# Early attention scores in pairs of sets on four 64x64 array tiles, value tiles kept by head pair, and a planner with other durations

## The chip, the cores and the metric

The kernel runs on one core of a Trainium2 chip. The metric is the device time of one launch in microseconds. The kernel before takes 553.24 us (median of 3 runs, 553.12 to 553.94).

## The reference, cut to what matters

Inputs: q, k, v of shape (2, 8, 768, 64): batch, heads, sequence, head width. Three stages follow one another, all in fp32.

```python
# 1. attention: banded local keys plus 24 summary keys (one for each block of 32)
k_sum = k.reshape(B, H, 24, 32, D).max(axis=3)
v_sum = v.reshape(B, H, 24, 32, D).mean(axis=3)
scores = concat(where(|i - j| < 16, scale * q @ k.T, -1e9), scale * q @ k_sum.T + log(32))
a = softmax(scores); x = a @ concat(v, v_sum)        # then (1536 tokens, 512)
# 2. h = x @ w_in (512 x 2048); g = h * tanh(softplus(h)); y = g @ w_out (2048 x 512)
# 3. out = ((y @ w1) * (y @ w2)) @ w3 @ w_out2
```

## The kernel before, in words

**Dense work.** The 1536 tokens are three blocks of 512 (n = 0, 1, 2). Each fp32 product of the dense stages is made of three matmuls on high and low parts (`mm3`, L103 to L106). Stage 2 goes by chunks of 128 hidden columns: `hidden` (12 matmuls of 128x512, written h) and `project` (12 more, written y). The weights come as 1 MB DMAs of 64-bit words and are decoded by `list_weight`: `shrink` (ACT or POOL), `low`, `sign` and `join` (DVE), `hi` (ACT) and `lo` (DVE), written c, dc.

**Attention.** One set is 256 tokens of one pair of heads of one batch: 24 sets in the order of `SETS`. A set has four groups of 64 queries; each sees 96 local keys and 24 summary keys, so a score row has 120 columns (`KW`). Sets 0 to 7 (`early`) are batch 0, tokens 0 to 511: together block n = 0, which the first h matmuls need. Sets 8 to 11 are (0, hp, 2), sets 12 to 15 (1, hp, 0), and sets 16 to 23 are (1, hp, 1) and (1, hp, 2), head pair by head pair.

- Early sets: keys of the whole batch lie in the tile `k`, queries in `qp`. `score` (L963) issues for each group and head one matmul on 96 keys and one on the 24 summary keys. The query group is the 64x64 weight; the two heads use the upper and the lower half of the array and write the two halves of the partitions of one PSUM bank. The banks are a ring of two (`a_ring`), one bank for a set.
- Late sets come in pairs: `score_two` (L978) writes the two heads to two banks and the two groups of a pair to the two halves of partitions, so that four 64x64 tiles of the array are in use. Their queries, keys and values come in one DMA (`load_late`, 624 KB) into `lt`, one of four tiles; `widen_k` and `widen_v` (POOL) write the 24 summary columns and rows beside them.
- After the scores: `peak` (DVE, four mask-and-max instructions, each with a read of its accumulator), `expo` (ACT, four exps), `invert` (DVE), `norm` (POOL), `turn_p` (PE, four transposes), `store_p` (ACT or DVE), `attend` or `attend_two` (PE), `store_x` (high part on ACT, low part on DVE; xh, xl).
- Summary values of batch 0: `parts_v` (PE, pn), `store_parts` (ACT, vq), `join_v` (PE, pm), `store_vm` (DVE, vm), `spread_v` (POOL). `peak_k` (DVE, km) makes the summary keys. The last four value groups of batch 0 are loaded by `load_vb` (256 KB) into the end of the same tile as the queries.

**Order.** No engine chooses at run time: each executes its instructions in the order in which they are issued. `op` lists every step with an engine, a duration, the keys it reads and writes, and a rank. `issue` then plans: a backward pass (`latest`) gives each step a latest start, a forward pass (`forward`) lets each engine take the ready step with the earliest one; eight rounds, the best is issued. All durations are the numbers in the `op` calls; `wait_after` holds the hand-over times between engines. While PE has had no h matmul yet, planned idle time is filled with `warm` matmuls on zeros; 12 more (`WARM`) stand at the start. The first 18 DMAs go in the written order `QUEUE`; all DMAs are issued by SP, in order.

Of the kernel before, what the change touches and what calls it, by code (L numbers as in the profile page):

```python
# [23 lines left out]
WARM = 12  # L24
# [40 lines left out]
def fused_kernel(  # L65
# [208 lines left out]
    def list_weight(key, u, rank, due, seng, heng, leng):  # L274
# [52 lines left out]
        op("pool" if seng == "pool" else "act", 1.1, due, [k], [d], shrink, table="exp" if prelu else None)  # L327
# [34 lines left out]
    def hidden(i, hbank):  # L362
# [443 lines left out]
    mask = cp.tile([P, 4, KW], F32, name="mask")  # L806
# [8 lines left out]
    def constants():  # L815
# [80 lines left out]
    def load_vb(hp):  # L896

        nc.sync.dma_start(out=vbs[hp].rearrange("p g d -> p (g d)"), in_=vw_d[hp, :, 8 * P:12 * P])

    def load_qp(hp):  # L900
        t = cp.tile([P, LW], F32, tag=f"lt{hp}", name=f"qp{hp}", bufs=1)
        qps[hp], vbs[hp] = t[:, 0:TB], t[:, LW - TB:].rearrange("p (g d) -> p g d", d=P)
        nc.sync.dma_start(out=qps[hp], in_=q_d[hp])

    def load_late(s):

        t = cp.tile([P, LW], F32, tag=f"lt{s % RS}", name=f"lt{s}", bufs=1)
# [58 lines left out]

    def score(s, key):
        sv = st[s]["sv"] = bank(key, f"s{s}")[:, 0:4 * KW].rearrange("p (g j) -> p g j", j=KW)
        b, hp, j = sets[s]
        for i in range(4):  # L970
            c = 256 * j + 64 * i
            for h in range(2):
                hs = slice(64 * h, 64 * h + 64)
                for c0, c1, x in ((0, 96, kts[b, hp][hs, c:c + 96]), (96, KW, kms[b, hp][hs])):
                    nc.tensor.matmul(
                        sv[hs, i, c0:c1], lhsT=qps[hp][hs, c:c + 64], rhs=x, start=True, stop=True,
                        skip_group_check=True,
                    )  # L978

    def score_two(s, keys):  # L980

        two = [bank(k, f"s{s}h{h}")[:, 0:4 * KW].rearrange("p (g j) -> p g j", j=KW) for h, k in enumerate(keys)]
        for w in range(2):
            x = st[s + w]
            x["sv"] = two
            for i in range(4):
                m, r = divmod(i, 2)
                for h in range(2):
                    hs = slice(64 * h, 64 * h + 64)
                    nc.tensor.matmul(  # L990
                        two[h][64 * r:64 * r + 64, 2 * w + m], lhsT=x["q"][hs, 64 * i:64 * i + 64],
                        rhs=x["k"][hs, i, :], start=True, stop=True, skip_group_check=True,
                    )

    def peak(s):
# [4 lines left out]
        for i in range(4):  # L1000
            if early(s):
                src, y = x["sv"][:, i, :], 1 if 4 * sets[s][2] + i else 0
            else:
                g = 4 * sets[s][2] + 2 * (i % 2)
                src, y = x["sv"][i // 2][:, 2 * (s % 2) + i % 2], {0: 2, 10: 3}.get(g, 1)
# [35 lines left out]
    def attend(s, key):  # L1041
        xb = bank(key, f"x{s}")
        b, hp, j = sets[s]
        for i in range(4):
            for h in range(2):
# [4 lines left out]
                    rhs=st[s]["pt"][:, i, hs], start=True, stop=True,  # L1050
# [51 lines left out]
    def list_keys(b, hp, rank, key):  # L1102
        kt = kt_key[b, hp] = held.get(key, key)
        op("dma", 1.1 if b else 1.15, rank, [], [kt], load_k, key, b, hp, late=QUEUE.get(f"k{b}{hp}"))
        op("dve", 0.9, rank, [kt], [("km", b, hp)], peak_k, b, hp)

    def list_means(b, hp, rank, ring):
# [6 lines left out]
        else:  # L1114
            op("dma", 0.75, rank, [], [("lt", hp)], load_qp, hp, late=QUEUE.get(f"q{hp}"))
            op("dma", 1.4, rank, [], [("va", hp)], load_va, hp, late=QUEUE.get(f"va{hp}"))
            op("dma", 0.72, rank, [("lt", hp)], [("ltv", hp)], load_vb, hp, late=QUEUE.get(f"vb{hp}"))
            k0, vq = ring.get(), ("vq", hp % 2)
            op("pe", 0.82, rank + 1.0, [("va", hp), ("lt", hp), ("ltv", hp), held["k0", hp]], [k0], parts_v, hp, k0)
            op("act", 0.3, rank + 1.0, [k0], [vq], store_parts, hp)  # L1120
            op("pe", 0.3, rank + 1.0, [vq], [key], join_v, hp, key)
        if b:
            op("act", 0.25, rank, [key], [("vm", b, hp), ("vmt", hp)], store_vm, b, hp)
        else:
            op("dve", 0.25, rank + 1.0, [key], [("vmt", hp)], store_vm, b, hp)
            op("pool", 1.4, rank + 1.0, [("vmt", hp), ("va", hp), held["k0", hp]], [("vm", b, hp)], spread_v, hp)

    def list_loads(s, rank):
        op("dma", 1.65, rank, [], [("lt", s % RS)], load_late, s)

    def list_score(s, rank, ring):
        if early(s):
            b, hp, j = sets[s]
            ks = [ring.get()]
            op("pe", 1.2, rank, [kt_key[b, hp], ("km", b, hp), ("lt", hp)], ks, score, s, ks[0])
            list_soft(s, rank, ks)
            return
# [25 lines left out]
    def list_attend(s, rank, ring):  # L1163
# [6 lines left out]
        else:  # L1170
            v = [(k, x % RS) for x in (s, s + 1) for k in ("lt", "ltv")]
            op("pe", 1.25, rank, [pt_key(s), pt_key(s + 1), *v], [kx], attend_two, s, kx)
        xs = {("x", n, hp)} if e else {("x", n, hp), ("x", n, place(s + 1)[1])}
        for part, eng in ((0, "act"), (1, "dve")):
# [3 lines left out]
            cost = ((0.34, 0.59), (0.42, 0.69))[part][not e]  # L1178
# [418 lines left out]
    def list_leave():  # L1597
        ks = [(x, i) for x in ("lt", "ltk", "ltv", "sc") for i in range(RS)] + [(x, i) for x in ("mx", "sm") for i in range(EARLY)]
# [19 lines left out]
    for s, t in enumerate(when):  # L1618
# [4 lines left out]
        second = not e and s % 2  # L1623
# [69 lines left out]
def layout(q, k, v, w_in, w_out, w1, w2, w3, w_out2):  # L1693
# [27 lines left out]
    for n in range(ng):  # L1721
# [4 lines left out]
            vw[b, hp, :, 4 * j:4 * j + 4].reshape(P, TB),  # L1726
# [6 lines left out]
        "late": late,  # L1733
        "v8": np.ascontiguousarray(v8.swapaxes(3, 4)).reshape(B, HP, P, 7 * P),
# [20 lines left out]
```

## Time and profile before

| | us |
|---|---|
| median of 3 runs | 553.24 |
| the profiled execution's own time | 555.6 |
| its span, first to last instruction | 553.9 |
| PE busy | 540.4 (98%) |
| DVE busy | 412.0 (74%) |
| ACT busy | 295.8 (53%) |
| POOL busy | 137.3 (25%) |
| mean granted PE clock, as a share of full speed | 0.997 |

How to read it: the profiled execution took 555.6 us by the clock that times the runs, 1.7 us more than its span. Matmuls are pipelined, so that the busy time of PE holds overlaps; its idle time is real. The chain that ended last consists of PE for 92%. A line such as L975 is a line of the kernel file; SPq is the queue from which DMAs are issued.

### The profile page before, as it was taken

How to read it: one execution, taken by the hardware profiler on the slowest of the kernel's cores; microseconds unless marked ns; L12 is line 12 of the kernel's file. 1: busy time of each engine (PE TensorE's matmuls, PEld its weight loads, DVE VectorE, ACT ScalarE, POOL GpSimd, SP SyncE). 2: the span in 40 equal slices, each digit the busy share in tenths (PEclk: the TensorE clock that was granted, in tenths of full speed). 3: DMA queues.
4: the chain of work that ended last, by engine and by line, in shares of the span. 5: the costliest groups of instructions: out<-in, count | busy, mean ns of one | idle time of the engine just before them, and what ended most of it. 6: DMA issues, size and time to landing. Idle time of an engine off the chain costs nothing.

```text
span 553.9 us, 8388 instructions
## 1 busy us (share of the span) xinstructions
PE 540.4 (98%) x3248; PEld 442.9 (80%) x3248; DVE 412.0 (74%) x682; ACT 295.8 (53%) x552; POOL 137.3 (25%) x156
## 2 busy tenths in 40 slices
PE   8969899999999999999999999999999999999997
PEld 7747678877888888888888888888888888888885
DVE  5899886233399994357798989799667588789892
ACT  4877698597643342336343447555345654434531
POOL 4662343222223135411511200000017333500000
PEclk9998999999999999999999999999999999999999
DMA  8996722222372000030406464422261342000003
GB/s 318 417 395 215 295 95 97 90 93 94 134 323 77 0 1 0 1 152 1 149 4 227 181 275 151 153 76 77 76 235 69 115 125 100 41 2 0 1 19 133
DMA packets 13863, 69.34 MB, mean 125 GB/s; under 512 B 1536, under 2 KB 1536, under 8 KB 8192
## 3 DMA queue, kind: packets, MB, share of 16 engines
q1 hardware_dynamic: 13824, 68.82, 33.2%
q8 instruction: 25, 0.41, 0.3%
q14 instruction: 14, 0.11, 0.1%
HBM read 65.67 MB, written 3.15 MB: 124 GB/s over the span
## 4 chain that ended last, share of the span: by engine, by line
PE 92%; DMA 2%; POOL 2%; DVE 2%; issue 1%; SPq 0%; POOLq 0%
PE y L104 8%; PE y L106 8%; PE y L105 8%; PE h L104 5%; PE h L105 5%; PE h L106 5%; PE s0g L549 3%; PE s0g L548 3%; PE wc L106 3%; PE wc L104 3%; PE s0g L547 3%; PE wc L105 3%; PE pt L1034 2%; PE z L1454 2%; PE z L1453 2%; PE z L1452 2%
## 5 line engine op out<-in xcount | busy, mean ns | idle before, releaser
L519 POOL TENSOR_TENSOR dw12p<-dw12p 128x256 f32<-128x256 f32 x32 | 33.5, 1047 | 132.5 <-DVE w12p L322 127.0
L393 DVE TENSOR_TENSOR gl<-e,gh 128x512 fp32r<-128x512 f32 x32 | 24.3, 764 | 39.7 <-ACT gh L389 39.7
L104 PE MATMUL h<-xh,c 128*128 128x512 f32 x128 | 52.4, 409 | 0.0
L104 PE MATMUL y<-gh,c 128*128 128x512 f32 x128 | 51.4, 401 | 0.0
L105 PE MATMUL h<-xl,c 128*128 128x512 f32 x128 | 50.4, 394 | 0.0
L106 PE MATMUL h<-xh,c 128*128 128x512 f32 x128 | 50.3, 393 | 0.0
L106 PE MATMUL y<-gh,c 128*128 128x512 f32 x128 | 50.0, 391 | 0.0
L105 PE MATMUL y<-gl,c 128*128 128x512 f32 x128 | 49.9, 390 | 0.0
L385 ACT ACTIVATE e<-h 128x512 f32<-128x512 f32 x32 | 19.2, 600 | 56.9 <-PE h L106 56.8
L1027 POOL TENSOR_TENSOR sc<-sc,sm 128x480 f32<-128x480 f32 x24 | 27.3, 1140 | 53.8 <-DVE sm L1023 31.9
L1015 ACT ACTIVATE sc<-sc,mx 128x120 f32<-128x120 f32 x96 | 36.6, 383 | 6.8 <-DVE mx L1006 6.7
L317 ACT CAST w<-dw 128x1024 fp32r<-128x1024 f32 x20 | 20.9, 1052 | 21.6 <-DVE dw L310 21.5
L104 PEld LDWEIGHTS h<-xh,c 128*128 128x128 f32 x128 | 24.3, 190 | 5.8 <-issue 0.8
L106 PEld LDWEIGHTS h<-xh,c 128*128 128x128 f32 x128 | 24.3, 190 | 5.3
L104 PEld LDWEIGHTS y<-gh,c 128*128 128x128 f32 x128 | 24.0, 188 | 5.4 <-issue 0.7
L106 PEld LDWEIGHTS y<-gh,c 128*128 128x128 f32 x128 | 24.0, 188 | 5.2
L105 PEld LDWEIGHTS h<-xl,c 128*128 128x128 f32 x128 | 24.3, 190 | 4.5
L105 PEld LDWEIGHTS y<-gl,c 128*128 128x128 f32 x128 | 24.1, 188 | 4.5
L310 DVE SCALAR_TENSOR_TENSOR dw<-dw,w 128x1024 int32<-128x1024 int32 x20 | 25.1, 1265 | 2.1 <-ACT dw L288 1.9
L788 DVE TENSOR_TENSOR ya<-y,ya 128x512 f32<-128x512 f32 x32 | 21.7, 687 | 6.6 <-PE y L106 6.5
L104 PE MATMUL wc<-w,w 128*128 128x512 f32 x64 | 24.9, 389 | 0.0
L105 PE MATMUL wc<-w,w 128*128 128x512 f32 x64 | 24.9, 389 | 0.0
(582 smaller groups left out, 1549.6 us busy)
## 6 DMA issues: line engine op xcount, KB each, us to landing
w<-in_w SPq DMA_DIRECT2D x20, 1024.0 KB, 4.9
c<-in_w SPq DMA_DIRECT2D x16, 1024.0 KB, 11.1
lt<-in_late SPq DMA_DIRECT2D x16, 624.0 KB, 4.8
w12p<-in_w SPq DMA_DIRECT2D x8, 1024.0 KB, 5.0
k<-in_vw SPq DMA_DIRECT2D x4, 512.0 KB, 8.7
out<-c SPq DMA_DIRECT2D x8, 256.0 KB, 2.0
v<-in_v SPq DMA_DIRECT2D x4, 448.0 KB, 8.5
k<-in_kt SPq DMA_DIRECT2D x4, 400.0 KB, 6.2
```

What stands on the lines that cost most here:

```text
L104: nc.tensor.matmul(o, lhsT=lh, rhs=rh, start=start, stop=False)
L105: nc.tensor.matmul(o, lhsT=lh, rhs=rl, start=False, stop=False)
L106: nc.tensor.matmul(o, lhsT=ll, rhs=rh, start=False, stop=stop)
L310: nc.vector.scalar_tensor_tensor(out=a, in0=a, scalar=3, in1=words(T["raw"])[0], op0=ALU.logical_shift_left, op1=ALU.bitwise_or,)
L317: (nc.scalar.copy if heng == "act" else nc.vector.tensor_copy)(t[:, 0], T["a"])
L385: nc.scalar.activation(T["e"], hb(), AF.Mish)
L393: nc.vector.tensor_tensor(out=T["gl"], in0=T["e"], in1=T["gh"].bitcast(F32), op=ALU.subtract)
L519: nc.gpsimd.tensor_tensor(out=quarter(o), in0=quarter(x), in1=quarter(y), op=sign)
L547: nc.tensor.matmul(B[b], lhsT=lh, rhs=yq[r][:, 0, kk], start=first and kk == 0, stop=False, skip_group_check=True)
L788: nc.vector.tensor_tensor(out=yacc[n][:, m], in0=banks[f"y{nm}_{m}"], in1=yacc[n][:, m], op=ALU.add)
L1015: nc.scalar.activation(x["sc"][:, i, :], x["sc"][:, i, :], AF.Exp, bias=x["mx"][:, i:i + 1], scale=-1.0, accum_out=sm[:, i:i + 1],)
L1027: nc.gpsimd.tensor_tensor(out=sc, in0=sc, in1=sm.unsqueeze(2).broadcast_to([P, 4, KW]), op=ALU.mult)
```

## The change

The early sets are scored in pairs by `score_two` too, two banks for a pair, with a 96-column and a 24-column matmul for each group and head; `attend` and `peak` read the new places, and the mask has three planes in place of four. The values leave the `lt` tile: each head pair has a value tile of its own (`vbs[hp]`), loaded by `load_vb` (96 partitions) for batch 0 and by the new `load_v` (192 KB) for batch 1; sets 8 to 11 find theirs there already, and `widen_v` runs for sets 8 to 15 alone. The last eight sets go token group by token group. The planner gets other durations, a term `port` for DVE and POOL steps that overlap, a start of `expo` 0.4 before the planned end of `peak`, and 9 in place of 12 first warm matmuls. Cut to the core:

```diff
-LOW = 0.7
+LOW = 0.6
+PORT = {"low", "sign", "join", "lo"}
-WARM = 12
+WARM = 9
-SETS += [(1, hp, j) for hp in range(HP) for j in (1, 2)]
+SETS += [(1, hp, j) for j in (1, 2) for hp in range(HP)]
-LW = 256 + 4 * KW + TB
+LW = 256 + 4 * KW
...
@@ forward
-            free[e] = end = t + ops[i][1]
+            end = t + ops[i][1]
+            if e == "pool" or e == "dve" and ops[i][5].__name__ in PORT:
+                end += max(0.0, min(end, port["dve" if e == "pool" else "pool"]) - t)
+                port[e] = end
+            free[e] = end
...
-                ready[d] = max(ready[d], end + wait_after(e, g))
+                ready[d] = max(ready[d], end + (-0.4 if ops[d][5].__name__ == "expo" and e == "dve" else wait_after(e, g)))
...
@@ list_weight
-            op("dve", 1.22, due, [k], [x], sign)
-        op("dve", 1.22, due, [k, x], [d], join)
-        op(heng, 0.98 if heng == "act" else 0.62, due, [d], [k], hi)
-        op(leng, 1.4 if leng == "dve" else 2.4, due, [d], [k], lo)
+            op("dve", 1.14, due, [k], [x], sign)
+        op("dve", 1.14, due, [k, x], [d], join)
+        op(heng, 0.96 if heng == "act" else 0.62, due, [d], [k], hi)
+        op(leng, 1.14 if leng == "dve" else 2.4, due, [d], [k], lo)
...
-        nc.sync.dma_start(out=vbs[hp].rearrange("p g d -> p (g d)"), in_=vw_d[hp, :, 8 * P:12 * P])
+        nc.sync.dma_start(out=vbs[hp][0:96].rearrange("p g d -> p (g d)"), in_=vw_d[hp, 0:96, 8 * P:12 * P])
...
-        qps[hp], vbs[hp] = t[:, 0:TB], t[:, LW - TB:].rearrange("p (g d) -> p g d", d=P)
+        qps[hp] = t[:, 0:TB]
+        vbs[hp] = cp.tile([P, 4, P], F32, tag=f"lv{hp}", name=f"vb{hp}", bufs=1)
...
-        st[s]["v"] = t[:, LW - TB:].rearrange("p (g d) -> p g d", d=P)
+        st[s]["v"] = vbs[s % RS]
...
+    def load_v(s):
+        b, hp, j = sets[s]
+        nc.sync.dma_start(
+            out=vbs[hp][0:96].rearrange("p g d -> p (g d)"), in_=v1_d[hp, j]
+        )
...
-        nc.gpsimd.tensor_copy(st[s]["v"][96:KW], vms[b, hp][96:KW].unsqueeze(1).broadcast_to([NB, 4, P]))
+        nc.gpsimd.tensor_copy(vbs[hp][96:KW], vms[b, hp][96:KW].unsqueeze(1).broadcast_to([NB, 4, P]))
...
@@ score_two (score is taken out)
+            b, hp, j = sets[s + w]
+            for n in range(16 if early(s) else 8):
+                h, r, m, y = n % 2, n // 2 % 2, n // 4 % 2, n // 8
+                i, hs = 2 * m + r, slice(64 * h, 64 * h + 64)
+                o = two[h][64 * r:64 * r + 64, 2 * w + m]
+                if early(s):
+                    c = 256 * j + 64 * i
+                    q = qps[hp][hs, c:c + 64]
+                    o = (o[:, 0:96], o[:, 96:KW])[y]
+                    k = (kts[b, hp][hs, c:c + 96], kms[b, hp][hs])[y]
+                else:
+                    q, k = x["q"][hs, 64 * i:64 * i + 64], x["k"][hs, i, :]
+                nc.tensor.matmul(o, lhsT=q, rhs=k, start=True, stop=True, skip_group_check=True)
...
-        op("dma", 1.1 if b else 1.15, rank, [], [kt], load_k, key, b, hp, late=QUEUE.get(f"k{b}{hp}"))
-        op("dve", 0.9, rank, [kt], [("km", b, hp)], peak_k, b, hp)
+        op("dma", 1.1 if b else 1.15 + 1.35 * (hp == 1), rank, [], [kt], load_k, key, b, hp, late=QUEUE.get(f"k{b}{hp}"))
+        op("dve", 0.86, rank, [kt], [("km", b, hp)], peak_k, b, hp)
...
@@ list_loads
-        op("dma", 1.65, rank, [], [("lt", s % RS)], load_late, s)
+        op("dma", 1.0, rank, [], [("lt", s % RS)], load_late, s)
+        if sets[s][0]:
+            op("dma", 0.55, rank + 0.01, [], [("lv", s % RS)], load_v, s)
...
@@ list_score
-            op("pool", 0.35, rank, [("lt", i), ("km", b, hp)], [("ltk", i)], widen_k, x)
-            op("pool", 0.8, rank, [("lt", i), ("vmt", hp)], [("ltv", i)], widen_v, x)
+            op("pool", 0.23, rank, [("lt", i), ("km", b, hp)], [("ltk", i)], widen_k, x)
+            if x < EARLY + 2 * HP:
+                op("pool", 0.58, rank, [("vmt", hp)], [("lvm", i)], widen_v, x)
...
-        op("pe", 1.2, rank, reads, ks, score_two, s, ks)
+        op("pe", 1.6 if early(s) else 1.2, rank, reads, ks, score_two, s, ks)
...
-        op("dve", 0.9, rank, ks, [small("mx", s), sc_key(s)], peak, s)
-        op("act", 1.68, rank, [small("mx", s)], [sc_key(s), small("sm", s)], expo, s, table="exp")
+        op("dve", 0.82, rank, ks, [small("mx", s), sc_key(s)], peak, s)
+        op("act", 1.53, rank, [small("mx", s)], [sc_key(s), small("sm", s)], expo, s, table="exp")
...
-        op("pool", 1.1, rank, [sm], [sc], norm, s)
+        op("pool", 0.95, rank, [sm], [sc], norm, s)
...
-            v = [(k, x % RS) for x in (s, s + 1) for k in ("lt", "ltv")]
+            v = [(k, x % RS) for x in (s, s + 1) for k in ("lv", "lvm")]
...
```

## Rows read from the trace of the kernel before

**Rows 1.** The page: busy time of each engine
```profile
PE 540.4 (98%) x3248; PEld 442.9 (80%) x3248; DVE 412.0 (74%) x682; ACT 295.8 (53%) x552; POOL 137.3 (25%) x156
```
**Rows 2.** Windows: stretch, length, busy PE, PEld, DVE, ACT, POOL, clock, DMA, GB/s
```profile
8.90:25.30 16.40, 15.79 (x345) 13.49 (x346) 13.33 (x80) 14.01 (x63) 8.51 (x8) 1.00 1.03 416
25.30:46.10 20.80, 15.65 (x208) 11.86 (x208) 19.71 (x43) 16.45 (x43) 14.59 (x14) 0.92 0.77 314
60.90:68.90 8.00, 6.11 (x30) 3.79 (x28) 5.81 (x6) 4.07 (x7) 5.50 (x6) 1.00 0.62 236
...
41.40:45.00 3.60, 3.35 (x10) 2.56 (x10) 3.60 (x4) 2.11 (x3) 3.54 (x4) 0.53 0.07 27
...
500.00:554.00 54.00, 50.29 (x222) 41.29 (x220) 40.21 (x49) 21.20 (x29) 0.00 (x0) 1.00 0.10 39
```
**Rows 3.** Chain of waits, in order of time: start us, us, what
```profile
11.04 1.26 PE s L975 x29
...
45.19 0.98 PE s10h L990 x32
```
**Rows 4.** Timeline to 24 us: start us, us, engine, line, operation, idle before
```profile
1.12 4.27 PE L813 MATMUL warm<-zero 128*128 128x128 f32 x24 [1.12 <-DVE zero L817]
3.81 0.95 DVE L916 TENSOR_REDUCE km<-k 128x24 f32<-128x768 f32 x1 [0.81 <-DMA k<-in_kt]
5.32 0.39 PE L975 MATMUL s<-k,qp 64*64 64x96 f32 x4
7.07 0.95 DVE L916 TENSOR_REDUCE km<-k 128x24 f32<-128x768 f32 x1 [2.31 <-DMA k<-in_kt]
7.94 0.27 DVE L1006 CUSTOM_DVE_ANT_0 sc<-s,mask 128x120 f32<-128x120 f32 x1
...
23.73 0.08 DVE L1006 DVE_READ_ACCUMULATOR2_ANT mx<- 128x1 f32 x1
```
**Rows 5.** Waits, of DVE to 70 us, of SP to 150: total, times, longest
```profile
DVE sc L1006 <- PE s L975: 1.5, 3, 0.6
...
SPq L911 <- PE x L1061: 66.5, 6, 19.4
```
**Rows 6.** Timeline of PE, 28 to 42 us: three of its five idle stretches
```profile
28.43 0.69 PE L1048 MATMUL x<-pT,k 120*64 120x64 f32 x16 [0.57 <-POOL k L954]
...
39.99 0.65 PE L1034 MATMUL pt<-ident,sc 128*120 128x128 f32 x4 [2.36 <-POOL sc L1027]
41.65 1.11 PE L1034 MATMUL pt<-ident,sc 128*120 128x128 f32 x4 [1.01 <-POOL sc L1027]
```
**Rows 7.** Timelines of POOL and DVE: norm of a set, lo of a weight
```profile
11.63 0.99 POOL L1027 TENSOR_TENSOR sc<-sc,sm 128x480 f32<-128x480 f32 x1 [6.12 <-ACT vq L941]
30.27 1.95 POOL L1027 TENSOR_TENSOR sc<-sc,sm 128x480 f32<-128x480 f32 x1
38.13 1.81 POOL L1027 TENSOR_TENSOR sc<-sc,sm 128x480 f32<-128x480 f32 x1 [3.20 <-ACT sc L1015]
40.67 2.01 DVE L322 TENSOR_TENSOR c<-dc,c 128x1024 fp32r<-128x1024 f32 x1
58.34 1.19 DVE L322 TENSOR_TENSOR c<-dc,c 128x1024 fp32r<-128x1024 f32 x1
```
**Rows 8.** The stop after 60 us: timelines of PE and POOL, chain of waits
```profile
62.84 0.65 PE L1034 MATMUL pt<-ident,sc 128*120 128x128 f32 x4 [1.32 <-POOL sc L1027]
65.78 0.65 PE L1034 MATMUL pt<-ident,sc 128*120 128x128 f32 x4 [0.57 <-POOL sc L1027]
...
60.88 0.52 POOL L965 COPY lt<-km 128x96 f32<-128x96 f32 x1 [15.85 <-DMA lt<-in_late]
...
52.73 8.00 DMA lt<-in_late
```
**Rows 9.** Timeline of PE, 138 to 140 us
```profile
138.48 0.40 PE L104 MATMUL h<-xh,c 128*128 128x512 f32 x1
139.96 1.15 PE L1061 MATMUL x<-pT,lt 120*64 120x64 f32 x32
```

More of the change, by code (lines that the diff above doesn't have):

```diff
@@ L71, in fused_kernel @@
     late_d: bass.AP,
+    v1_d: bass.AP,
     v8_d: bass.AP,
@@ L164, in forward @@
         idle = True
+        port = {"dve": 0.0, "pool": 0.0}
         def rank_of(i):
@@ L326, in list_weight @@
         prelu = seng == "prelu"
-        op("pool" if seng == "pool" else "act", 1.1, due, [k], [d], shrink, table="exp" if prelu else None)
+        op("pool" if seng == "pool" else "act", 1.06, due, [k], [d], shrink, table="exp" if prelu else None)
         x = ("low", *k)
@@ L396, in hidden @@
         R = i + 0.9
-        op("act", 0.53, R, [hbank], [e], s0, table="mish")
-        op("act", 0.56, R, [hbank], [gh], s1, table="mish")
-        op("dve", 0.66, R, [e, gh], [gl], s2)
+        op("act", 0.5, R, [hbank], [e], s0, table="mish")
+        op("act", 0.5, R, [hbank], [gh], s1, table="mish")
+        op("dve", 0.6, R, [e, gh], [gl], s2)
         return T
@@ L805, in fused_kernel @@
     ident = cp.tile([P, P], F32, name="ident")
-    mask = cp.tile([P, 4, KW], F32, name="mask")
+    mask = cp.tile([P, 3, KW], F32, name="mask")
     cw = cp.tile([96, 2 * NB + 6], F32, name="cw")
@@ L833, in constants @@
             )
-        for i in (0, 2, 3):
+        for i in (0, 2):
             nc.vector.tensor_copy(mask[:, i, :], mask[:, 1, :])
-        nc.vector.memset(mask[:, 0, 0:WIN], NEG / scale)
-        nc.vector.memset(mask[0:64, 2, 0:WIN], NEG / scale)
-        nc.vector.memset(mask[64:P, 3, 96 - WIN:96], NEG / scale)
+        nc.vector.memset(mask[0:64, 0, 0:WIN], NEG / scale)
+        nc.vector.memset(mask[64:P, 2, 96 - WIN:96], NEG / scale)
         def bands(t, n, lo, step):
@@ L965, in widen_k @@
         nc.gpsimd.tensor_copy(st[s]["k"][:, :, 96:KW], kms[b, hp].unsqueeze(1).broadcast_to([P, 4, NB]))
[L967 to L978, printed above, removed]
     def score_two(s, keys):
@@ L985, in score_two @@
             x["sv"] = two
[L986 to L993, printed above, removed]
+            b, hp, j = sets[s + w]
[11 more added lines that the diff above has]
+                nc.tensor.matmul(o, lhsT=q, rhs=k, start=True, stop=True, skip_group_check=True)
     def peak(s):
@@ L1000, in peak @@
         for i in range(4):
[L1001 to L1005, printed above, removed]
+            g = 4 * sets[s][2] + 2 * (i % 2)
+            src, y = x["sv"][i // 2][:, 2 * (s % 2) + i % 2], {0: 0, 10: 2}.get(g, 1)
             nc.vector.tensor_tensor_reduce(
@@ L1049, in attend @@
                     xb[hs, 64 * i:64 * i + 64], lhsT=kvs[hp][0:KW, c:c + 64],
-                    rhs=st[s]["pt"][:, i, hs], start=True, stop=True,
+                    rhs=st[s]["pt"][:, 2 * h + i // 2, 64 * (i % 2):64 * (i % 2) + 64], start=True, stop=True,
                 )
@@ L1116, in list_means @@
             op("dma", 1.4, rank, [], [("va", hp)], load_va, hp, late=QUEUE.get(f"va{hp}"))
-            op("dma", 0.72, rank, [("lt", hp)], [("ltv", hp)], load_vb, hp, late=QUEUE.get(f"vb{hp}"))
+            op("dma", 0.72, rank, [], [("lv", hp)], load_vb, hp, late=QUEUE.get(f"vb{hp}"))
             k0, vq = ring.get(), ("vq", hp % 2)
-            op("pe", 0.82, rank + 1.0, [("va", hp), ("lt", hp), ("ltv", hp), held["k0", hp]], [k0], parts_v, hp, k0)
-            op("act", 0.3, rank + 1.0, [k0], [vq], store_parts, hp)
+            op("pe", 0.82, rank + 1.0, [("va", hp), ("lv", hp), held["k0", hp]], [k0], parts_v, hp, k0)
+            op("act", 0.17, rank + 1.0, [k0], [vq], store_parts, hp)
             op("pe", 0.3, rank + 1.0, [vq], [key], join_v, hp, key)
         if b:
-            op("act", 0.25, rank, [key], [("vm", b, hp), ("vmt", hp)], store_vm, b, hp)
+            op("act", 0.28, rank, [key], [("vm", b, hp), ("vmt", hp)], store_vm, b, hp)
         else:
             op("dve", 0.25, rank + 1.0, [key], [("vmt", hp)], store_vm, b, hp)
-            op("pool", 1.4, rank + 1.0, [("vmt", hp), ("va", hp), held["k0", hp]], [("vm", b, hp)], spread_v, hp)
+            op("pool", 1.0, rank + 1.0, [("vmt", hp), ("va", hp), held["k0", hp]], [("vm", b, hp)], spread_v, hp)
     def list_loads(s, rank):
-        op("dma", 1.65, rank, [], [("lt", s % RS)], load_late, s)
+        op("dma", 1.0, rank, [], [("lt", s % RS)], load_late, s)
+        if sets[s][0]:
+            op("dma", 0.55, rank + 0.01, [], [("lv", s % RS)], load_v, s)
     def list_score(s, rank, ring):
[L1132 to L1137, printed above, removed]
         reads = []
@@ L1177, in list_attend @@
             begun.add((part, n))
-            cost = ((0.34, 0.59), (0.42, 0.69))[part][not e]
+            cost = ((0.27, 0.48), (0.34, 0.61))[part][not e]
             own = [("x%d" % part, *x[1:]) for x in sorted(xs)]
@@ L1597, in list_leave @@
     def list_leave():
-        ks = [(x, i) for x in ("lt", "ltk", "ltv", "sc") for i in range(RS)] + [(x, i) for x in ("mx", "sm") for i in range(EARLY)]
+        ks = [(x, i) for x in ("lt", "ltk", "lv", "lvm", "sc") for i in range(RS)] + [(x, i) for x in ("mx", "sm") for i in range(EARLY)]
         ks += [("kt", i) for i in range(2)] + [("pt", i) for i in range(4)] + [(x, i) for x in ("v8", "vs") for i in range(2)]
@@ L1622, in fused_kernel @@
         t0 = t - (1.6 if e else 1.8)
-        second = not e and s % 2
+        second = s % 2
         if (b, hp) not in started:
@@ L1632, in fused_kernel @@
             at_time(t, list_score, s, t, rings[0])
-        t1 = t + (1.2 if e else 0.9 + 0.5 * second)
+        t1 = t + (1.2 if e else 0.9 + 0.5 * (s % 2))
         at_time(t1, list_turn, s, t1, rings[1])
-        if not second:
+        if e or not second:
             at_time(done[s], list_attend, s, done[s], rings[2])
@@ L1725, in layout @@
             qt[b, hp, :, 256 * j:256 * j + 256], kw[b, hp, :, 4 * j:4 * j + 4].reshape(P, 4 * KW),
-            vw[b, hp, :, 4 * j:4 * j + 4].reshape(P, TB),
         ], axis=1) for b, hp, j in SETS[EARLY:]
@@ L1733, in layout @@
         "late": late,
+        "v1": np.stack([vw[1, :, 0:96, 4 * j:4 * j + 4].reshape(HP, 96, TB) for j in range(3)], axis=1),
         "v8": np.ascontiguousarray(v8.swapaxes(3, 4)).reshape(B, HP, P, 7 * P),
```

9 lines of the change are left out of this document (6 added, 3 removed).

## The prediction, made before the changed kernel ran

> **What bounds the kernel now.** First the page's engine line: PE is busy 540.4 us of a span of 553.9 [rows 1], so 13.5 us of idle time are all that waiting can give back; the rest is matmuls, which only fewer or better packed ones shorten. Then the windows, to see where PE idles: 0.6 us in 8.9 to 25.3, 5.2 in 25.3 to 46.1, 1.9 in 60.9 to 68.9 and 3.7 in the last 54 [rows 2]; what is left lies before 8.9. Beside these stands one fall of the granted clock, to 0.53 in 41.4 to 45.0 [rows 2], behind idle stretches of 2.36 and 1.01 us [rows 6]. So the change can act on the first 69 us; from there on PE is full, and whatever the front gains arrives whole at the end. In the front the chain of waits is to be read next: from 8.9 to 25.3 it runs nearly all on PE, and the scores of seven early sets are its largest part [rows 3]; behind 25.3 it alternates between POOL, DVE and PE. DVE is busy 19.7 of 20.8 us there and ACT 14.0 of 16.4 before [rows 2]: two engines stand close behind PE.
>
> **A, the front up to the peaks of set 7.** An early set's scores take 1.26 us of PE, a late pair, two sets on four tiles, 0.98 [rows 3]. An early pair will have 32 matmuls (64 records in the trace) where the late pair has 16 (32 records). Bounds: 1.26 if four tiles halve what two tiles take (2 x 1.26 / 2); 1.96 if each record keeps the late pair's pace (0.98 / 32 x 64). No row shows the mix; I take 1.6, the middle. PE then spends 4 x 1.6 = 6.4 in place of 8 x 1.26 = 10.1, 3.7 less (2.2 to 5.1).
>
> [...]
>
> What of it reaches the path? Set 0's peak starts at 7.94, although its scores began at 5.32 and take 1.26: DVE had first the summary keys of head pair 1, whose data came at 7.07 [rows 4]. The planner now counts 1.35 more for that load and so puts the peaks first. The 9 warm matmuls end at 1.12 + 4.27 x 9 / 12 = 4.32, the first summary keys at 3.81 + 0.95 = 4.76 [rows 4]; scores from about 4.95, pair done at 6.6, peak of set 0 at about 6.85, 1.1 earlier. But a pair holds both banks: the next pair's scores wait for both peaks, and its peaks for all 1.6 us of its scores. Two peaks take 1.64, a hand-over 1.6 + 0.28 + 0.2 = 2.1 (the last two are the planner's hand-over times). If PE and DVE alone set the pace, the last peak ends at 6.85 + 4 x 1.64 + 3 x 2.1 = 19.7, against 23.8 now [rows 4]: -4.1. DVE also has other work in this stretch, 13.33 busy less six sets' peaks of 0.82 (the planner's new number), 8.4 us [rows 2]; if all of it stands ahead of the last peak and covers the hand-overs, the peak ends at 6.85 + 6.56 + 8.4 = 21.8. If none of it falls into the hand-overs, DVE idles 6.3 there where it idles 1.5 now [rows 5]: +4.8. I take 22.1, near the DVE bound, since the planner fills DVE's waits with ready work: **-1.7** (-4.1 to +4.8).
>
> **B, from there to full PE at 46.1.** PE idles 5.15 us here and loses about 1.7 to the clock (3.6 us at 0.53 are 1.9 at 1.00) [rows 2]: 6.8 at most. The change names causes for a part: two norms took 1.95 and 1.81 where one took 0.99, and a lo 2.01 where another took 1.19 [rows 7], each beside work of the other engine of DVE and POOL; the long ones are 2.6 us over. The planner now counts such overlaps, and its durations are nearer to the rows (expo, norm, peak). If that order avoids them, PE's idle stretch of 2.36 [rows 6] shrinks and with it the cause of the clock's fall. Of 2.6 + 1.7 = 4.3 I take three quarters: **-3.2** (-6.8 to +2.4, one more stretch as long as today's longest).
>
> **C, the stop at 60.9 to 65.8.** POOL sat 15.85 us in `widen_k` of set 12, whose data were issued at 52.73, behind set 8's attend, and took 8.00 [rows 8]; a norm queued behind it cost PE 1.32 + 0.57 = 1.89. In the new kernel `lt` holds queries and keys alone, so the load waits for the scores of set 8, not for its attend, and is 368 KB, not 624. I take two thirds, **-1.3** (-1.9 to 0; no more work comes into that wait).
>
> **What costs nothing.** `load_v` is 12 more issues on SP; it waits for the attend of four sets earlier, as the whole `lt` load does now (66.5 us of waiting [rows 5]), and the weights behind it in SP's order are in no worse place. Bytes fall by 4 x 64 KB (`vb`) and 4 x 256 KB (sets 8 to 11): 1.3 MB, about 3 us at 416 GB/s [rows 2]. I give no gain: DVE and ACT decode the first weights late, not DMA. Eight `widen_v` fewer on POOL, one mask copy fewer on DVE before the first key comes: beside idle time. The new set order makes block 2's first two head pairs complete only with the attend that now stands at 139.96; its h matmuls begin at 138.48 [rows 9]. The six that stand between these two, 1.5 us, must in part move behind it; y matmuls cover this, and without that cover it costs up to 1.5.
>
> **Sum.** -1.7 - 3.2 - 1.3 = -6.2 against the profiled execution's 555.6 (span 553.9 and 1.7 around it), so 549.4. That execution is 2.4 us above the median of 553.24; the same step from the median gives **547.0**.
>
> **The rivals.**
> 1. Slower: the pair that holds both banks. DVE's hand-overs stay uncovered (+4.8 in A), the waits of B only move along behind DVE's later queue (0), C holds (-1.3): +3.5, 556.7. For it: ring of two banks, both taken by each pair. Against it: 8.4 us of other DVE work for 6.3 us of hand-overs. If B holds, it decides only beyond 1.5 + 3.2 + 1.3 = 6.0 us of idle hand-overs.
> 2. Nothing comes of it: DVE, busy 95% in 25.3 to 46.1, sets the start of full PE; A's gain ends in its queue, B and C trade one stall for another: -0.5, 552.7. For it: the DVE share; against it: 2.6 us of that share are stretched instructions.
> 3. The plan fits: A at -2.6 (nearer to the PE and DVE pace), B at -5.6, C at -1.9: -10.1, 543.1. For it: every PE idle stretch in the front ends in a POOL or DVE wait; against it: DVE and ACT have little room.
> 4. The change does not do what it says: the four tiles do not overlap and a pair takes 2.5 us, so A gives nothing and B and C hold: -4.5, 548.7. Against it: the late pair's 0.98 [rows 3].
>
> **How the numbers follow.** Forecast 0.50 (own range 544.8 to 550.5), rival 1 0.16, rival 2 0.14, rival 3 0.13, rival 4 0.07. A measurement of this kernel tells about 0.2%, 1.1 us, from no change. Faster: forecast, rivals 3 and 4, and a third of rival 2: 0.75; within 0.2%: most of the rest of rival 2, 0.09; slower: 0.16. The range goes from 541.5, past rival 3, to 555.0, which takes in rival 2 and the lesser half of rival 1.
>
> **What would show it.** A: score pieces of about 1.6 us for a pair, the first peak near 6.9, the last early peak near 22; DVE's waits for scores show the hand-overs. B: PE full from about 41 rather than 46, norms near 1.0, no fall of the clock. C: no idle PE behind a norm near 60. The forecast is wrong if full PE starts later than 45, or if a new idle stretch of PE above 2 us stands behind 69.

## The result, and the profile after

The changed kernel takes 556.62 us (median; 555.45 to 556.98) where the kernel before takes 553.24: ratio 1.0052, 95% interval 1.0038 to 1.0067. It is slower, by some 2.9 us; 547.0 was forecast. The profiled executions are 556.75 (span 555.1) and 555.6 (span 553.9), so between the two traces only 1.2 of the 2.9 us can be found: the one shown of before lies 2.4 above its median. A second trace of the kernel before (run e0 below, 554.73) helps out.

First the windows of the changed kernel, which answer to [rows 2]. Columns: stretch, length, busy PE, PEld, DVE, ACT, POOL, granted clock, DMA share, GB/s.

```profile
8.90:25.30 16.40, 13.44 (x351) 10.47 (x349) 14.48 (x72) 12.19 (x60) 9.53 (x10) 1.00 1.03 338
25.30:46.10 20.80, 15.41 (x174) 11.73 (x171) 18.27 (x42) 15.44 (x40) 12.61 (x12) 0.83 0.89 358
60.90:68.90 8.00, 8.00 (x39) 5.88 (x38) 6.98 (x9) 6.66 (x9) 0.92 (x2) 1.00 0.75 249
```

Four things are to be seen. In the first window PE is 2.35 us less busy than before: the pairs do save PE time, and it is idle time now (about 1.0 of it goes with the narrow load below: with wide loads PE is busy 14.47). There, too, the DMA engines are as fully occupied as before (1.03) and move 338 GB/s in place of 416. In the second window PE idles 5.4 us as it did (5.2), and the mean clock is 0.83, not 0.92. In the third there is no stop after 60 us.

The last two of these need the second trace of the kernel before, whose second and third window are:

```profile
25.30:46.10 20.80, 15.67 (x192) 11.91 (x195) 19.67 (x44) 16.38 (x43) 14.65 (x14) 0.87 0.76 311
60.90:68.90 8.00, 8.00 (x68) 5.72 (x66) 7.38 (x9) 5.71 (x8) 5.59 (x6) 1.00 0.73 270
```

The kernel before, too, runs without the stop after 60 us: there PE is late by 1.3 us when it gets to that place, since it ran 6.83 us at half clock (40.84 to 47.67) where [rows 2] has some 3.4. In a third trace of the same order (run e2 below, narrow loads) the clock does not fall in this stretch at all, and the stop after 60 us is 2.65 us long. In these three traces, the longer the half clock, the shorter the later stop.

The timeline of PE in the front answers to [rows 4]. Columns: start, length, engine, line, operation, count, in brackets the idle time before and what ended it.

```profile
5.21 0.56 PE L998 MATMUL s0h<-k,qp 64*64 64x96 f32 x16
...
6.15 0.38 PE L998 MATMUL s0h<-km,qp 64*64 64x24 f32 x16
...
9.11 0.56 PE L998 MATMUL s2h<-k,qp 64*64 64x96 f32 x16
...
10.05 0.38 PE L998 MATMUL s2h<-km,qp 64*64 64x24 f32 x16
...
20.82 0.18 PE L998 MATMUL s6h<-km,qp 64*64 64x24 f32 x1 [1.35 <-issue]
```

A pair takes 1.32 us (5.21 to 6.53, 9.11 to 10.43), where one set took 1.26. In the middle of the last early pair PE stops for 1.35 us and nothing in the profile releases it. Now DVE in the same stretch, where the peaks of sets 0 to 3 are:

```profile
6.58 0.28 DVE L1008 CUSTOM_DVE_ANT_0 sc<-s0h,mask 128x120 f32<-128x120 f32 x1 [1.83 <-PE s0h L998]
...
8.20 0.95 DVE L929 TENSOR_REDUCE km<-k 128x24 f32<-128x768 f32 x1
...
10.07 0.53 DVE L1024 TENSOR_SCALAR sm<-sm 128x4 f32<-128x4 f32 x1 [0.63 <-ACT sc L1017]
...
11.68 0.95 DVE L929 TENSOR_REDUCE km<-k 128x24 f32<-128x768 f32 x1 [0.86 <-DMA k<-in_kt]
12.55 0.27 DVE L1008 CUSTOM_DVE_ANT_0 sc<-s2h,mask 128x120 f32<-128x120 f32 x1
...
23.26 0.09 DVE L1008 DVE_READ_ACCUMULATOR2_ANT mx<- 128x1 f32 x1
```

The first peak stands at 6.58, 1.36 earlier than before; the last early peak ends at 23.35, only 0.46 earlier. The scores of sets 2 and 3 are done at 10.43, but their peaks start at 12.55: DVE's order has the summary keys of head pair 2 ahead of them, and their data come late.

Then the stretch in which the time is lost: PE, POOL and DVE of the changed kernel from 39 us on, against [rows 6, 7].

```profile
39.73 0.40 PE L108 MATMUL h<-xh,c 128*128 128x512 f32 x1
42.51 1.03 PE L1036 MATMUL pt<-ident,sc 128*120 128x128 f32 x4 [2.38 <-POOL sc L1029]
44.43 1.11 PE L1036 MATMUL pt<-ident,sc 128*120 128x128 f32 x4 [0.89 <-POOL sc L1029]
45.19 0.77 PE L106 MATMUL h<-xh,c 128*128 128x512 f32 x1
```
```profile
40.38 4.00 POOL L1029 TENSOR_TENSOR sc<-sc,sm 128x480 f32<-128x480 f32 x2 [5.28 <-DVE sm L1024]
```
```profile
37.79 1.22 DVE L317 SCALAR_TENSOR_TENSOR dc<-dc,c 128x1024 int32<-128x1024 int32 x1
...
40.41 1.20 DVE L317 SCALAR_TENSOR_TENSOR dc<-dc,c 128x1024 int32<-128x1024 int32 x1
41.52 3.94 DVE L329 TENSOR_TENSOR c<-dc,c 128x1024 fp32r<-128x1024 f32 x2
```

The stop that the new order was to remove is there, 2.5 us later: the norms of sets 8 and 9 and the lo of weight chunks 1 and 2 lie side by side, and the norms take twice, the lo 1.7 times as long as alone (0.99 and 1.19 in [rows 7]). PE has no other work: chunk 0's last h matmul is at 39.73, and chunk 1 is not decoded before 43.5. The granted clock in the two stretches at half speed:

```profile
28.98:32.40 3.42, 3.42 (x52) 3.12 (x51) 3.36 (x5) 0.69 (x2) 2.77 (x3) 0.50 1.01 409
42.64:49.46 6.82, 5.93 (x42) 4.48 (x45) 5.37 (x5) 5.35 (x7) 1.74 (x1) 0.50 0.34 114
```

Each fall (1.00 to 0.50) stands behind an idle stretch of PE: 1.29 us before 28.09 and 2.38 before 42.51. Before, the clock fell once in this stretch, for 3.4 us in the trace of [rows 2] and for 6.83 in e0. So the second fall here is as long as one that the kernel before has too; the first is new.

The 80th matmul of 512 columns (67.44 us in the changed kernel) comes 0.94 us later than in the trace of before, and from the 350th (151.33) to the last the distance is 0.9 throughout; against e0 it is 1.83 at the 80th and 1.7 to the end. All is decided in the first 68 us, and the sets' new order costs nothing.

### The profile page after: what moved, and what is told of

It reads as the page before. It is cut to its first block, busy times and chain, and to the rows that moved or that the text cites. A ratio compares the mean times of both kernels' runs of the same rounds, so it can differ in the third digit from the quotient of the medians.

```text
span 555.1 us, 8458 instructions
## 1 busy us (share of the span) xinstructions
PE 541.7 (98%) x3264; PEld 442.8 (80%) x3264; DVE 411.8 (74%) x680; ACT 298.2 (54%) x554; POOL 136.4 (25%) x148
## 4 chain that ended last, share of the span: by engine, by line
PE 92%; DVE 3%; DMA 3%; issue 1%; POOL 0%; ACT 0%; SPq 0%
PE y L106 8%; PE y L108 8%; PE y L107 8%; PE h L106 6%; PE h L108 5%; PE h L107 5%; PE s0g L554 3%; PE s0g L555 3%; PE wc L108 3%; PE wc L106 3%; PE s0g L556 3%; PE wc L107 3%; DMA k<-in_kt 3%; PE z L1455 2%; PE z L1454 2%; PE z L1456 2%
## 5 line engine op out<-in xcount | busy, mean ns | idle before, releaser
L400 DVE TENSOR_TENSOR gl<-e,gh 128x512 fp32r<-128x512 f32 x32 | 24.7, 774 | 42.8 <-ACT gh L396 42.8
L329 DVE TENSOR_TENSOR w<-dw,w 128x1024 fp32r<-128x1024 f32 x20 | 25.1, 1258 | 0.4 <-ACT w L324 0.2
```

Source lines behind the costliest of these rows:

```text
L329: e.tensor_tensor(out=t[:, 1], in0=T["a"], in1=t[:, 0].bitcast(F32), op=ALU.subtract)
L400: nc.vector.tensor_tensor(out=T["gl"], in0=T["e"], in1=T["gh"].bitcast(F32), op=ALU.subtract)
```

## The experiments

All ratios are to the kernel before, timed beside it on the same chip, with 95% intervals. The runs come from several chips; comparing two ratios assumes that a chip moves all these kernels alike. "lo 1" is the end of the decode of weight chunk 1 in the profiled execution; PE's h matmuls of that chunk wait for it.

| run | scores | planner's numbers | `vb` partitions | us | ratio (interval) | lo 1 |
|---|---|---|---|---|---|---|
| e0 before | single | old | 128 | 554.46 | 1.0005 (0.9993 to 1.0017) | 42.8 |
| e2 | single | old | 96 | 554.89 | 1.0026 (1.0010 to 1.0043) | 43.5 |
| e5 | single | new | 128 | 549.32 | 0.9912 (0.9893 to 0.9931) | 36.7 |
| changed | pairs | new | 96 | 556.62 | 1.0052 (1.0038 to 1.0067) | 43.5 |
| e1 | pairs | new | 128 | 555.53 | 1.0029 (1.0015 to 1.0042) | 42.3 |
| e3 | pairs | old | 96 | 553.58 | 0.9999 (0.9977 to 1.0020) | 43.4 |
| e4 | pairs | old | 128 | 551.70 | 0.9966 (0.9948 to 0.9984) | 39.7 |
| e7 | single | old | 128 | 550.82 | 0.9942 (0.9922 to 0.9962) | 39.0 |
| e9 | single | new | 128 | 549.75 | 0.9927 (0.9912 to 0.9943) | 37.6 |
| e6 | pairs | new, no overlap term | 128 | 554.81 | 1.0019 (1.0002 to 1.0036) | 41.5 |
| e8 | pairs | new, chunk 1 sooner | 128 | 553.43 | 0.9994 (0.9981 to 1.0007) | 38.6 |
| e10 | pairs | new, warm in the stop | 128 | 553.09 | 0.9994 (0.9982 to 1.0006) | 41.6 |

e0, e2 and e5 are the kernel before with one part of the change at most; the others are the changed kernel (late value tiles kept, new set order).

**The narrow load.** Only the rows of `vb` that are loaded are changed: in e1 back to 128 in the changed kernel, in e2 to 96 in the kernel before. e0 is the kernel before itself.

```
-        nc.sync.dma_start(out=vbs[hp][0:96]..., in_=vw_d[hp, 0:96, 8 * P:12 * P])
+        nc.sync.dma_start(out=vbs[hp]..., in_=vw_d[hp, :, 8 * P:12 * P])
```

> The kernel before, once more, to have its spans and clocks run by run and a second trace. 553.2 us. If the stretch of half clock behind the stop for the norms of sets 8 and 9 is what sets its single executions apart (the profiled one took 555.6, the median 553.24), the runs near 553 show a mean clock of 0.998 or more and those near 555 show 0.997. The rate of the loads in 8.9 to 25.3 us should again be near 416 GB/s; if it is near 340 here too, the slow loads of the changed kernel were chance and not the change.

> The changed kernel, with only the four early value loads going to all 128 partitions again (256 KB, not 192), the order of every engine being the same. Theory 1, slow loads: a 96-partition load among the others slows all transfers around it, so the rate in 8.9 to 25.3 us rises from 338 to about 410 GB/s, the last early value load lands 2.5 us sooner, and the kernel takes about 554 (2 to 3 us less). Rival 1, the order: nothing moves, 556.6, since the first decode of weights is late by the order on DVE. Rival 2, pairs: nothing moves either, since PE's stops without a releaser (1.35 and 1.29 us) come from its doubled rate of instructions.

> The kernel before, with only the four early value loads cut to 96 partitions, the order being the same. Theory 1, slow loads: the rate in 8.9 to 25.3 us falls from 416 towards 340 GB/s and the kernel takes 2 to 3 us more, about 556. Rivals 1 and 2: no change, 553.2, or 0.5 less for the 0.25 MB that are not moved.

The windows of e1 and, behind it, of e2 (columns as above):

```profile
8.90:25.30 16.40, 14.47 (x359) 11.46 (x358) 15.34 (x77) 13.60 (x68) 9.56 (x11) 1.00 1.03 414
25.30:46.10 20.80, 15.37 (x173) 11.43 (x174) 19.80 (x43) 16.35 (x38) 12.35 (x12) 0.88 0.75 304
```
```profile
8.90:25.30 16.40, 14.98 (x330) 12.63 (x330) 13.41 (x77) 12.96 (x60) 8.40 (x8) 1.00 1.03 342
```

Four loads of 96 partitions take the rate of this whole window from 416 to 342 GB/s in the kernel before, and it comes back to 414 where they are widened again, at the same DMA share. Other loads slow down with them: the 512 KB loads of `k` land 9.7 us after their issue in e2, against 8.7 before. That shows the cause of the slower transfers, though not how they come to be slower. The time follows by 1.2 us (e2 less e0, by the ratios), 1.3 (changed less e1) and, under the old numbers, 1.8 (e3 less e4): three times the same sign, though the two intervals overlap each time. Expected were 2 to 3 us.

**The planner's numbers.** e3 and e4 are the changed kernel (96 and 128 rows) with the planner's durations of before, 12 first warm matmuls and neither the overlap term nor the early exps (the costs of the new loads and of a pair stay); e5 is the kernel before with the new ones; e6 is e1 without the overlap term alone. Shown: e5's edits in short, and e6's.

```
-LOW = 0.7
+LOW = 0.6
...
-        op("dve", 0.9, rank, ks, [small("mx", s), sc_key(s)], peak, s)
+        op("dve", 0.82, rank, ks, [small("mx", s), sc_key(s)], peak, s)
...
-            if e == "pool" or e == "dve" and ops[i][5].__name__ in PORT:
+            if e in ():
```

> The changed kernel planned with the durations of the kernel before (no overlap term, no early start of the exps, 12 first warm matmuls). Rival 1, the order: the new durations are what cost; with the old ones the pairs and the smaller loads give their gain, 549 to 552. Theory 1, slow loads: the loads are as slow as in the changed kernel (about 340 GB/s in 8.9 to 25.3 us), 555 to 558. Rival 2, pairs: the stops of PE without a releaser stay above 1 us, 555 to 558.

> The changed kernel with the planner's old durations and with the early value loads on 128 partitions: both suspects undone, pairs and value tiles kept. Theory 2: slow loads cost 1.3 us and the order from the new durations 2.9, and they add up; then this takes 1.4 us less than the kernel before, a ratio of about 0.9975. Rival, no addition: the sooner loads end in the same waits behind POOL and DVE, ratio 0.999 to 1.001.

> The kernel before with only the planner's numbers changed (durations, overlap term, early exps, 9 warm matmuls); early sets scored one by one, values in the late tiles, loads on 128 partitions. Theory 2: the new numbers make a worse order whatever the scores are, ratio about 1.005 (556.5). Rival: they hurt only with the pairs, whose two banks leave the planner no room, ratio 0.995 to 1.000.

> The changed kernel with loads on 128 partitions and the planner's overlap term for DVE and POOL left out, all other new numbers kept; to be read against the one with the term (ratio 1.0029). If the term makes the order worse, the ratio falls to 0.998 to 1.000 and the stop before the transposes of sets 8 and 9 (2.4 us and 0.9) shrinks. If the shorter durations or the early exps do, the ratio stays at 1.002 to 1.004 and the stop stays.

The new numbers gain 0.9%, 4.9 us, in the kernel before (e5) and lose 3.5 with pairs (e4 to e1: 0.9966 to 1.0029, intervals apart). For e5 a loss was expected, or a gain of at most 0.5%; both were wrong. e3 fell between its expectations, e4 came as expected. e6 tells that the overlap term is not what loses: without it 1.0019, within e1's interval. Nor is it the stretched decode alone: the three lo of chunks 0 to 2 take 5.2 us in e1, and 3.8 in e6, with the same time. First e1's, then e6's row (8.9 to 46.1; busy, mean ns of one, idle before):

```profile
L329 DVE TENSOR_TENSOR c<-dc,c 128x1024 fp32r<-128x1024 f32 x3 | 5.2, 1748 | 0.1
```
```profile
L329 DVE TENSOR_TENSOR c<-dc,c 128x1024 fp32r<-128x1024 f32 x3 | 3.8, 1273 | 0.1
```

Nor is it the stop before the transposes of sets 8 and 9 alone. In e6 that stop is down to 0.26 us, and the 20th matmul of 512 columns starts at 44.0, 4.7 us sooner than in e1; by the 350th nothing of that is left (150.08 against 150.01). So the time went with the one expectation and the stop with the other. Part of the gain goes into a later stop of the kind of [rows 8] and 3.4 us at half clock behind it: POOL waits in `widen_k` for a late set's data, and PE for the norm behind it, although the `lt` loads are the small ones here. POOL, then PE:

```profile
68.73 0.27 POOL L978 COPY lt<-km 128x96 f32<-128x96 f32 x1 [1.81 <-DMA lt<-in_late]
...
69.75 1.84 POOL L1029 TENSOR_TENSOR sc<-sc,sm 128x480 f32<-128x480 f32 x1
```
```profile
71.64 0.65 PE L1036 MATMUL pt<-ident,sc 128*120 128x128 f32 x4 [2.50 <-POOL sc L1029]
```

e5 also shows what sets full PE. Its last early peak ends at 25.6, 2.5 us later than e1's (23.1), and yet its 20th matmul of 512 columns starts at 40.5 in place of 48.7: lo 1 is at 36.7 in place of 42.3. Its windows:

```profile
8.90:25.30 16.40, 16.40 (x353) 13.91 (x351) 14.63 (x78) 14.34 (x62) 8.74 (x9) 1.00 1.03 417
25.30:46.10 20.80, 17.74 (x216) 12.75 (x215) 20.10 (x63) 18.05 (x46) 12.70 (x14) 1.00 0.81 317
60.90:68.90 8.00, 8.00 (x62) 6.46 (x62) 7.79 (x27) 7.71 (x22) 2.18 (x3) 1.00 0.64 241
```

Here PE is full in the first window, and in the second it works 2.4 us more than in e1. In the third window there is no stop; but as e0, the kernel before itself, has none there either and e6 has one at 69 to 72 us, no run tells whether the numbers or the smaller `lt` loads would remove it.

**The pairs.** e7 and e9 are e4 and e1 with the single-set `score` of before in place of early pairs; the tiles that are kept and the set order stay those of the change, and the mask gets its fourth plane back for them.

```
+            if early(s):
+                src, y = x["sv"][:, i, :], 3 if 4 * sets[s][2] + i == 0 else 1
...
+            op("pe", 1.2, rank, [kt_key[b, hp], ("km", b, hp), ("lt", hp)], ks, score, s, ks[0])
...
-        second = s % 2
+        second = not e and s % 2
```

> Old durations, loads on 128 partitions, values by head pair, but the early sets scored one by one as in the kernel before; to be read against the same with pairs. If the pairs gain what they save on PE (1.26 for a set against 1.2 for a pair, 5 us in all, of which the path keeps a third), this is 1 to 2 us slower than with pairs. If the hand-over of both banks eats the gain, it is the same or up to 1 us faster.

> The changed kernel with its new numbers and value tiles, but early sets scored one by one and loads on 128 partitions: the parts that gained, put together. Theory 3 has the pairs cost only through the order that the planner makes with them; without them the new numbers gained 4.5 us in the kernel before (ratio 0.9912) and the value tiles should add 1 us (no stop at 60): ratio 0.988 to 0.991, the fastest so far. Rival: both gains are the same stop, ratio 0.991 to 0.994.

Pairs cost 1.3 us with the old numbers (e4 less e7, intervals overlapping) and 5.6 with the new ones (e1 less e9, intervals far apart). So most of it is not the pair as such but the order that the planner makes of it. The 1.3 go with the clock: e7's six executions all have a mean granted clock of 0.998 or more (median 550.8), and the six of e4's twelve that have it too take as long (550.6). e7 was expected to lose, or to gain at most 1 us; e9 met its rival's range. PE of e9 in the stretch where the changed kernel stops, then DVE:

```profile
37.52 0.39 PE L106 MATMUL h<-xh,c 128*128 128x512 f32 x1
...
39.59 0.60 PE L1053 MATMUL pt<-ident,sc 128*120 128x128 f32 x4
...
41.61 0.65 PE L1053 MATMUL pt<-ident,sc 128*120 128x128 f32 x4 [0.72 <-POOL sc L1046]
```
```profile
36.44 1.21 DVE L329 TENSOR_TENSOR c<-dc,c 128x1024 fp32r<-128x1024 f32 x1
...
39.52 1.20 DVE L317 SCALAR_TENSOR_TENSOR dc<-dc,c 128x1024 int32<-128x1024 int32 x1
```

lo 1 runs ahead of the norms and alone (1.21), and PE has chunk 1's h matmuls to do while POOL norms sets 8 and 9 (one idle stretch of 0.72). In the changed kernel join 2 and the low of chunk 2 stand before lo 1 on DVE, and lo 1 falls beside the norms. The kernel before has that order too (join 2 at 37.90, lo 1 at 40.67), and so have e0, e1, e2 and e10; in the other runs lo 1 comes first, with pairs (e3, e4, e6, e8) or without. So neither the pairs nor the numbers bring it about alone.

**Chunk 1 sooner, and the clock.** e8 lets the planner take the decode steps of chunk 1 as due one chunk sooner; e10 puts matmuls on zeros (7 and 3) ahead of the transposes of sets 8 and 9, which fill the stop.

```
-(zero - b) / CHUNK
+(zero - b) / CHUNK - 1.0 * (i in sooner)
...
+        for _ in range({8: 7, 9: 3}.get(s, 0)):
+            nc.tensor.matmul(pb[:, 0:P], lhsT=zero, rhs=zero, start=True, stop=True)
```

> The changed kernel with loads on 128 partitions, all its new numbers kept, and one thing more: the planner takes the latest start of the decode steps of weight chunk 1 one chunk (5.4 us) sooner. To be read against the same without it (ratio 1.0029; join of chunk 1 at 36.5 us, its lo at 40.2 to 42.3, PE full from about 45). Theory 3: what sets full PE is the decode of chunk 1 on DVE, which the new order put behind the peaks of sets 8 and 9 and behind the join of chunk 2; with it sooner, its lo ends before 38, PE is full from about 41 and the ratio falls to 0.990 to 0.996. Rival, bank hand-over: the pairs themselves cost by holding both banks; the ratio stays at 1.001 to 1.004.

> The changed kernel with loads on 128 partitions and ten matmuls on zeros (seven before the transposes of set 8, three before those of set 9) in PE's idle time there, nothing else moved. To be read against the same without them (ratio 1.0029, half clock for 6.83 us from 41.3). If the half clock behind the stop costs what PE does in it, it does not fall there, and the time falls by 1.5 to 3 us, ratio 0.997 to 1.000. Rival: PE waits for decoded weights there anyway and the clock costs nothing: ratio 1.002 to 1.004.

e10 first: PE's timeline there, then the windows 41.27 to 48.10 of e10 and of e1.

```profile
38.01 1.72 PE L1036 MATMUL pt<-zero 128*128 128x128 f32 x14
40.55 0.65 PE L1038 MATMUL pt<-ident,sc 128*120 128x128 f32 x4 [0.81 <-POOL sc L1029]
...
42.47 0.65 PE L1038 MATMUL pt<-ident,sc 128*120 128x128 f32 x4 [0.60 <-POOL sc L1029]
```
```profile
41.27:48.10 6.83, 6.23 (x60) 4.88 (x59) 6.79 (x22) 5.71 (x10) 1.15 (x1) 1.00 0.34 90
```
```profile
41.27:48.10 6.83, 6.01 (x42) 4.57 (x46) 5.44 (x5) 5.37 (x8) 1.83 (x1) 0.50 0.24 75
```

With the stop filled the clock stays at 1.00 and the kernel is 1.9 us faster (1.0029 to 0.9994, intervals apart), as expected. In the two traces, e10 is ahead by 0.68 us at the first matmul of 512 columns and by 2.94 from the 20th on, so that 2.3 us come in this stretch: the half clock behind the stop costs about that much. A second reading agrees. Of 94 executions of the kernel before, timed beside these runs, 8 have a mean granted clock of 1.000 (median 552.1 us), 34 one of 0.995 to 0.997 (553.4) and 51 one of 0.993 or 0.994 (554.3): some 7 us at half clock go with 2.2 us. At the same clock e1 and the kernel before are alike (0.993: medians 554.4 and 554.3); but every execution of e1 has that clock or a lower one.

e8 brings lo 1 to 38.6 and gains the same 1.9 us, about half of the smallest gain expected. By the 20th matmul of 512 columns it is 7.1 us ahead of e1 in the traces, by the 350th only 1.2. Before that it has a fall of the clock that e1 has not, at 19.82, at the end of a stop inside an early pair; PE, then the first window:

```profile
19.98 0.19 PE L1001 MATMUL s6h<-km,qp 64*64 64x24 f32 x1 [1.16 <-issue]
```
```profile
8.90:25.30 16.40, 14.90 (x327) 12.03 (x326) 14.07 (x71) 11.70 (x58) 9.72 (x11) 0.83 1.03 412
```

Behind it the gain went into later stops: lo 2 ends at 45.8 (43.8 in e9), and PE idles 0.68 us in 46.1 to 60.9 and 0.64 in 60.9 to 68.9, where e1 has none:

```profile
46.10:60.90 14.80, 14.12 (x119) 10.62 (x116) 14.13 (x33) 14.57 (x34) 5.51 (x6) 1.00 0.87 334
60.90:68.90 8.00, 7.36 (x86) 5.41 (x86) 6.99 (x25) 7.92 (x23) 4.29 (x2) 1.00 0.98 341
```

So the theory "full PE waits for lo 1" fits the order of the table (lo 1 before 40: 549.3 to 551.7; after 41: 553.1 to 556.6) with e8 as the exception, but it is not shown to be the cause: in e8 and e6 PE is full sooner and most or all of the gain is lost again to later waits and to the clock.

## Why the prediction was wrong

The step that failed is **B**, "if that order avoids them, PE's idle stretch of 2.36 [rows 6] shrinks and with it the cause of the clock's fall". The order did not avoid them. The norms took 2.00 on average, the lo 1.97, PE's idle stretches are 2.38 and 0.89, and the clock is at half for 6.83 us there, as in e0; none of the 3.2 us forecast for this term came. I counted three quarters of what a well informed planner could win; but new numbers are only good together with the work they order. They won 4.9 us in the kernel before and lost 3.5 with pairs. The link from the stop to the clock was too simple as well: behind the same stop of 2.36 and 1.01 us the kernel before lost 3.4 us at half clock, or 6.83 (e0), or none (e2, the same order).

**What costs nothing** failed too: "I give no gain: DVE and ACT decode the first weights late, not DMA". I counted the bytes saved and not the shape of the transfer. The narrow load costs 1.2 to 1.8 us, as far as overlapping intervals tell.

**A** was right in its sizes on PE and wrong in what arrives. Its pair of 1.32 us is under the 1.6 that I took, and near the lower of its bounds, 1.26. The first peak came at 6.58 (6.85 forecast), the last ended at 23.35 (22.1). Its gain of 0.5 says little about the end: in e5 and e3 the last early peak ends latest (25.6), and e5 has the lowest time. I added A to B as if both lay on one path, while PE's first full stretch begins with h matmuls that wait for DVE's decode of chunk 1.

**C** looks right, since the stop after 60 us is gone, but that is luck. The term was read off one execution: e0, the same kernel, has no such stop, and e6, with the smaller loads of the change, has one of 2.50 us at 69. Nor could it be added to B: in the three traces of the old order the stop comes where the clock lost least, so that B and C were in part the same time.

**The rivals.** Rival 1 gave 556.7, and 556.62 was measured, but not by its mechanism: the hand-over of both banks does not show. DVE waits for scores once, 1.83 us before the first peak, where no bank is handed over; its other waits before 12 us, 0.63 and 0.86, end with ACT and a DMA. PE waits once for a bank that the peaks hold, 0.99 at 13.95, where it waited 1.15 at 8.93 in the trace of before. Rival 2 had the mechanism, "DVE sets the start of full PE; A's gain ends in its queue", and not the loss.

The sum by ratios, in us: without pairs and narrow load the change is worth -4.0 (e9); pairs with the order made for them +5.6, of which about 1.9 is the clock behind the stop; the narrow load +1.3. That makes +2.9, as it must, since the parts are the steps of one chain of runs (before, e9, e1, changed). Which parts of the change cost is shown; open is by which waits the pairs' order loses the other 3.7 us. A stop of PE of 1.1 to 1.7 us without a releaser inside an early pair is in every run with pairs (inside single scores at most 0.8, in e9). In e3 and e8 the clock fell to half for 6.83 us at the end of such a stop (1.69 and 1.16), in the other five traces it did not fall there; so the stop can cost, and what makes it was not tried. The best versions run are e5 and e9, both with single early scores and both faster than the two kernels of the case; with intervals that overlap, neither is shown better.

## What to carry to other kernels

PE time saved in a stretch where another engine set the pace became idle time here (8.9 to 25.3 us: PE busy 14.47 in e1 in place of 15.79), and an idle PE also lost its clock (0.50 for 6.8 us behind 2.38 us without work): before crediting a gain, find the step that the next full stretch waits for (here, most likely, the decode of one weight chunk), ask what the change does to that one, and look whether a later wait takes the gain back. Credit a stop only if a second trace of the same kernel has it too. A planner's new durations and new work must be timed apart and together: the numbers alone won 0.9%, with pairs they lost. Keep a load's partition count when trimming its bytes, or time the trimmed load (96 in place of 128 took the rate from 416 to 342 GB/s here).

## What the runs showed of the hardware

- Loads of 96 of 128 partitions slowed the transfers around them here: 416 to 342 GB/s over 16.4 us for four loads of 192 KB, at a full DMA share (kernel before and e2; 338 in the changed kernel, 414 with 128 partitions again in e1); fewer bytes, more time.
- In the changed kernel two norms on POOL and, on DVE, a join and two lo, 5.6 us if run alone one by one (2 x 0.99 + 1.20 + 2 x 1.19), took 5.1 side by side (40.38 to 45.46): here two engines were hardly faster than one. The norm that starts at 40.38, beside the join of 40.41 (1.20 us), takes 2.08 us and ends 0.85 us behind it; what stretches it is not shown.
- The same idle stretches of PE, 2.36 and 1.01 us, were followed by 3.4 us at half clock (before), 6.83 us (e0) or none (e2); in the changed kernel 1.29 us were followed by 3.4 and 2.38 by 6.8. A fall cost less than half its length here: filling the stop with matmuls on zeros gave back 1.9 us of 6.83 (e10), and in the kernel before some 7 us at half clock go with 2.2 us.
- Stops of TensorE of 1.06 to 1.69 us without a releaser stand inside a run of small matmuls on four 64x64 tiles in all seven traces with early pairs; on two tiles the longest inside the scores is 0.79 (e9).
